# A fused attention and two-layer kernel whose setup loads x later, spreads its products differently and starts the second attention earlier

## The chip, the cores and the metric

The kernel runs on one core of one Trainium2 chip. The metric is device time in microseconds (us) of the whole launch. Before the change three runs gave a median of 1218.57 us (1217.18 to 1219.75).

## What is computed

From the reference, cut to what matters (B, H, S, Ns, D = 8, 8, 512, 32, 64):

```python
scores = scale * x @ state.T;  a = softmax(scores);   xread = a @ state
scores2 = scale * state @ x.T; a2 = softmax(scores2); sread = a2 @ x
x = concat([xread, sread], axis=2)          # 8 blocks of 512 + 32 rows, 512 wide
x = ((x @ w1) * (x @ w2) @ w3) @ w_out      # w1, w2: 512 x 1024; w3: 1024 x 1024; w_out: 1024 x 512
h = x @ w_in;  out = (h * clip(h + 3, 0, 6) / 6) @ w_out2
```

All tensors come in single precision; the weights are handed over as 64-bit words that the kernel converts itself.

## The kernel before, in words

**Setup.** Twenty units of 1 MB (128x4096 of 16 bits) are loaded by SyncE (SP), and ScalarE (ACT) and VectorE (DVE) turn each into a 128x1024 fp32 tile. `ORDER` (line 120) gives their kinds: units 0 to 7 alternate w_out (`o`) and the first half of w3 (`a`), 8 to 11 are the second half of w3 (`w`), 12 to 19 are w1 and w2 (`p`). `Pipe.pump` (line 194) does unit t: three DVE instructions (`ts`, `hd`, then a product, lines 164 to 166), a hook `inside(t)`, the last DVE instruction (line 168), then ACT's `hd` of unit t+1 (line 151) and SP's load of unit t+3 (three `raw` buffers, so a load waits for the product of the unit three before). After that `more(t)` issues what is written there for step t: loads of x (`load_x`), steps of the attention generator, ends of w3 rows (`w3_done`), products of w3 by w_out (`bulk_mm`, line 463, tiles `ps_w`), and from t = 15 on the work of block 0.

**The folded weight.** `bulk_mm(n)` takes up to n of the 64 fp32 products of w3 @ w_out; eight of them add up to one of eight rows m = 0 to 7 in a PSUM bank of four (`ps_w`). `w3_done(m)` splits row m into a high and a low part (`w3ph` by ACT, `w3pl` by DVE) and so frees the bank. Later products are done as three passes on such parts (`mm3`, lines 88 to 90).

**Attention of a block.** `attention(b, fine)` is a generator: load `xn`; `scores` 0 (line 237); out of it (`mr`, `sN`, `e`: lines 241 to 244); scores 1; out of it; `max_n` (286 to 289); `exp_n` (292, 294); `e2_t` 0 (transposes, line 252); `sum_n`; `e2_t` 1; `div_n`; `sread` (267); `turn` (306); `Ah`; `Al`. `step()` advances the oldest living generator by one piece. With `fine` true (the attentions of blocks 0 and 1) each of these is a step of its own. The results `Ah`, `Al` are what block b multiplies by.

**P.** Instead of x @ w1 the kernel forms P = state @ w1 (w2) for four parts v per block (`p_mm`, line 409, tiles `ps_p`, two PSUM banks of a second set of four) and splits it (`p_split`, tiles `ph`, `pl`).

**Block 0 inside the setup.** `early_mm(m)` (12 products into two banks `ps_ab`), `early_ab(m)` (`asb` by ACT, `ab` by DVE, then `abh` by ACT and `abl` by DVE) and `early_x2(m)` (12 products by w3's row m into `x`) do slots 0 to 3 of block 0 at t = 16 to 20. Slots 4 to 7 and the blocks after that go through `slot(b, m, ...)`, with one attention step ahead of `ab`'s parts (`before`) and one after (`mid_`).

**The second stream.** `stream2()` (line 475) is a generator that converts and splits the weights of the last layer during blocks 0 to 5; `ROOM` and, for block 0, `ROOM0` say how much of it each of a slot's two hooks may take. Its first step loads two units, its second is ACT's `hd` (line 489), its third DVE's `ts` (line 516).

All engines run in the order in which this program issues; nothing reorders it.

Of the kernel before, what the change touches and what calls it, by code (L numbers as in the profile page):

```python
# [19 lines left out]
def attn_moe_kernel(tc, xt_d, xn_d, bd_d, wa, wb, wc, wi, wo, out):  # L20
# [36 lines left out]
    def close_pool(key):  # L57
        es.pop(key).close()
# [4 lines left out]
    def acc_bank(name):  # L63
        return psum.tile([128, 512], F32, tag="acc", name=name, bufs=4)
# [55 lines left out]
    ORDER = "oaoaoaoawwwwpppppppp"  # L120

    ROOM = ((3, 3), (3, 4), (3, 3), (3, 3), (0, 1), (3, 3), (5, 5), (5, 6))
    ROOM0 = (None, None, None, None, (0, 0), (1, 2), (2, 3), (2, 3))


    class Pipe:
# [87 lines left out]
    def load_x(b):  # L214
        xr = att.tile([128, 4, 512], F32, tag="xr", name=f"xr{b}")
        br = mid.tile([128, 4, 64], F32, tag="br", name=f"br{b}", bufs=2)
        nc.sync.dma_start(out=br, in_=bd_d[b])
        nc.sync.dma_start(out=xr, in_=xt_d[b])
        x_t[b] = (xr, br)
# [153 lines left out]
    live = []  # L373

    def step():
        if live:
            try:
                next(live[0])
            except StopIteration:
                live.pop(0)  # L380
# [5 lines left out]
    with tc.manual_schedule():  # L386
# [26 lines left out]
        def p_split(v):  # L413
            ps = p_ps.pop(v)
            h, l = (main.tile([128, 2, 512], F32R, tag=f"p{hl}", name=f"p{hl}", bufs=2) for hl in "hl")
            for i in range(2):
                phl[v, i] = h[:, :, 256 * i:256 * i + 256], l[:, :, 256 * i:256 * i + 256]
            for c in range(2):
                rnd(h[:, c], ps[c], "A")
            for c in range(2):  # L420
                rest(l[:, c], ps[c], h[:, c], "V")

        def w3_out(m, ps):
            w3p_h[m], w3p_l[m] = w3p_tile("h", m), w3p_tile("l", m)
            rnd(w3p_h[m], ps, "A")
            rest(w3p_l[m], ps, w3p_h[m], "V")
# [31 lines left out]
        def bulk_mm(n):  # L458
            for _ in range(min(n, len(bulk))):
                t, m, k, o = bulk.pop(0)  # L460
                if k == 0:
                    w3_ps[m] = acc_bank(f"ps_w{m}")
                nc.tensor.matmul(w3_ps[m], t[:, o:o + 128], wout[k], start=k == 0, stop=k == M1 - 1)
# [98 lines left out]
        def w3_done(m):  # L562
            w3_out(m, w3_ps.pop(m))
# [24 lines left out]
        def x2_mm(blk, m, ab, n, es_):  # L588
            if m == 0 and es_[0] == 0:
                accs[blk] = [acc_bank(f"x2_{e}") for e in range(KD)]  # L590
            for e in es_:
                mm3(accs[blk][e][:, :n], w3p_h[m][:, e * 128:(e + 1) * 128], w3p_l[m][:, e * 128:(e + 1) * 128],
                    ab[0][:, :n], ab[1][:, :n], m == 0, m == M1 - 1)
# [140 lines left out]
        def early_x2(m):  # L734
            x2_mm(0, m, e_ab[m], 512, range(4))


        def early_ab(m):
            ab = ab_mul(*e_ps.pop(m), 512)
            hi = ab_hi(ab, 512)  # L740
            e_ab[m] = hi, ab_lo(ab, hi, 512)

        def inside(t):
            if t == 16:
                p_split(0)
            elif t > 16:
                if t == 17:
                    w3_done(7)
                early_ab(t - 17)
                if t == 17:  # L750
                    p_split(1)

        def more(t):
            if t == 1 or t == 12:
                load_x(t // 12)
            if t in (4, 18):
                live.append(attention(t // 18, True))
                step()
            for _ in range({5: 1, 6: 1, 7: 1, 8: 1, 10: 1, 11: 1, 12: 2, 13: 1, 19: 1}.get(t, 0)):
                step()  # L760
            for m in {9: (0, 1), 10: (2, 3), 11: (4,), 13: (5,), 15: (6,)}.get(t, ()):
                w3_done(m)
            if t == 15:
                p_mm(0)
            if t in (4, 5, 9, 10, 11):
                step()
            if t > 1 and ORDER[t] in "aw":
                w3u[ORDER[:t].count("a") + ORDER[:t].count("w")].mm()
            if t >= 16:
                early_mm(t - 16)  # L770
            bulk_mm(4 if t == 1 or t > 8 else 5 if t < 8 else 3)
            if t == 16:
                p_mm(1)
            if t >= 17:
                early_x2(t - 17)
            if t == 18:
                step()
            if t == 19:
                p_mm(2)

# [11 lines left out]
        early_ab(3)  # L792
        p_split(2)
        early_x2(3)
        second = stream2()
        for b in range(B):
            if 0 < b < B - 1:
                live.append(attention(b + 1))
            if b == B - 2:
                for _ in second:  # L800
                    pass
                close_pool("cvs")
                wsq = open_pool("wsq", bufs=1, side=right, reuse_waits="tile")
            if b == B - 1:
                xs_h, xs_l = xs_hl
                s_block()
                close_pool("wsq")
                close_pool("att")
                xb = open_pool("xb", bufs=1, side=right, reuse_waits="tile")
                first = combos(0)  # L810
            A = A_t.pop(b)
            for m in range(0 if b else 4, M1):
                if m == (6 if b else 5) and b + 2 < B:
                    load_x(b + 2)

                def pump(i):
                    nonlocal room
                    room += (ROOM if b else ROOM0)[m][i]
                    while room > 0:
                        room -= next(second, 99)  # L820

                def before():
                    step()
                    pump(0)

                vn = 4 * b + m // 2 + 1

                def mid_():
                    if vn < 4 * B and m % 2 == 0:
                        p_mm(vn)  # L830
                        p_split(vn)
                    step()
                    pump(1)
                slot(b, m, A, before, mid_)
                if b == 0:
                    step()
                if b == B - 2 and m >= 2:
                    if m == 2:
                        xs_r = wsq.tile([128, KD, SR], F32, name="xs_r")
                        n = (B - 1) * NS  # L840
                        nc.sync.dma_start(out=xs_r[:, :, :n], in_=xsd[:, :, :n])
                    ws_split(m - 2, [wsq.tile([128, 1024], F32R, tag=f"ws{hl}", name=f"ws{hl}", bufs=6) for hl in "hl"])
                if b == B - 1:
                    for _ in range(1 if m == 0 else 4):
                        next(first, None)
            drain_att()
# [476 lines left out]
```

## Time and profile before

| | value |
|---|---|
| median of 3 runs | 1218.57 us (1217.18 to 1219.75) |
| the profiled execution | 1216.74 us; its span, first to last instruction, 1214.9 us |
| TensorE (PE) busy | 1188.6 us, 98% of the span |
| VectorE busy | 861.2 us, 71% |
| ScalarE busy | 552.8 us, 46% |
| chain that ended last | PE 90%, DVE 7%, DMA 1%, ACT 1% |
| mean granted TensorE clock | 0.995 of full speed |

The shares are means over stages. A wait is read from the row of the instruction that waited: in brackets stands how long its engine sat idle before it, and who released it. A matmul's start times are exact, its end is modelled, so the distance from one start to the next is the better measure of one matmul.

### The profile page before, as it was taken

To read this page: it belongs to the slowest core of one execution; us is meant where nothing else is said; L and a number is where in the kernel's file an instruction comes from. 1 tells how busy PE (TensorE), PEld (TensorE's weight loads), DVE (VectorE), ACT (ScalarE), POOL (GpSimd) and SP (SyncE) were. 2 spreads that over 40 slices of the span, in tenths; PEclk is the share of its full clock that TensorE was granted. 3 is DMA by queue.
4 is the path that set the end of the run, shared out by engine and by line. 5 is a ranking of instruction groups with operands and counts; after the bars stand their busy time and mean duration, and the time that the engine had idled before them with its cause. 6 is when DMAs were issued, how large, how long until landed. Compare 5 with 4: busy or idle time off the path is not lost.

```text
span 1214.9 us, 17239 instructions
## 1 busy us (share of the span) xinstructions
PE 1188.6 (98%) x6734; PEld 945.8 (78%) x6734; DVE 861.2 (71%) x1230; ACT 552.8 (46%) x811; POOL 44.6 (4%) x59
## 2 busy tenths in 40 slices
PE   7898899999999999999999999999999999999998
PEld 4445677778777779978888888888888888888887
DVE  6986589888978664264678866688666886558483
ACT  3533455654645454244445434455344543334341
POOL 0000000000000000000101001010010100001100
PEclk9999899999999999999999999999999999999999
DMA  9761358675765511126899778898788986445973
GB/s 345 248 249 69 115 192 260 206 262 192 257 213 193 198 51 38 51 96 216 250 273 266 248 258 258 262 263 257 254 258 261 263 256 226 162 142 161 249 231 70
DMA packets 118930, 252.67 MB, mean 208 GB/s; under 512 B 45248, under 2 KB 63168, under 8 KB 112448
## 3 DMA queue, kind: packets, MB, share of 16 engines
q1 hardware_dynamic: 109552, 222.46, 53.9%
q0 software_dynamic: 7632, 27.79, 11.4%
q10 hardware_dynamic: 1664, 1.31, 0.3%
q8 instruction: 53, 0.87, 0.3%
q14 instruction: 29, 0.24, 0.1%
HBM read 182.39 MB, written 47.64 MB: 189 GB/s over the span
## 4 chain that ended last, share of the span: by engine, by line
PE 90%; DVE 7%; DMA 1%; ACT 1%; issue 0%; SPq 0%; ACTq 0%; DVEq 0%
PE ps L995 25%; PE ps_d L1157 25%; PE x L88 5%; PE x L89 5%; PE x L90 5%; PE ps_ab L88 5%; PE ps_ab L89 5%; PE ps_ab L90 5%; PE ps_p L409 3%; PE ps_hs L995 2%; PE ps_so L1170 2%; DMA raw<-in_wb_dram 1%; PE ps_r L267 1%; PE ps_s L237 1%; DVE t L168 1%; DVE big L168 1%
## 5 line engine op out<-in xcount | busy, mean ns | idle before, releaser
L995 PE MATMUL ps<-xc,wah 128*128 128x512 f32 x512 | 157.9, 389 | 0.0
L79 DVE TENSOR_TENSOR hlj<-g,hlj 128x1024 fp32r<-128x1024 f32 x84 | 102.2, 1217 | 35.6 <-ACT hlj L71 32.6
L925 ACT ACTIVATE rl<-c,half 128x512 f32<-128x512 f32 x96 | 69.5, 724 | 117.0 <-DVE c L895 68.1
L995 PE MATMUL ps<-xc,wbh 128*128 128x512 f32 x384 | 118.3, 389 | 0.0
L1157 PE MATMUL ps_d<-hlj,wah 128*128 128x512 f32 x384 | 118.2, 389 | 0.0
L88 PE MATMUL x<-abh,w3ph 128*128 128x512 f32 (+1 forms) x288 | 112.2, 390 | 0.0
L71 ACT ACTIVATE hlj<-g 128x1024 fp32r<-128x1024 f32 x84 | 88.5, 1057 | 50.7 <-PE ps_d L1157 45.2
L995 PEld LDWEIGHTS ps<-xc,wah 128*128 128x128 f32 x512 | 95.7, 188 | 19.5
L89 PE MATMUL x<-abl,w3ph 128*128 128x512 f32 (+1 forms) x288 | 109.3, 379 | 0.1
L90 PE MATMUL x<-abh,w3pl 128*128 128x512 f32 (+1 forms) x288 | 108.9, 378 | 0.0
L89 PE MATMUL ps_ab<-Al,ph 128*128 128x512 f32 x256 | 101.2, 395 | 2.4 <-DVE Al L79 2.4
L88 PE MATMUL ps_ab<-Ah,ph 128*128 128x512 f32 x256 | 102.7, 401 | 0.6 <-ACT Ah L71 0.4
L90 PE MATMUL ps_ab<-Ah,pl 128*128 128x512 f32 x256 | 101.0, 395 | 0.0
L995 PE MATMUL ps<-xc,wal 128*128 128x512 f32 x256 | 99.6, 389 | 0.0
L1157 PE MATMUL ps_d<-hlj,wbh 128*128 128x512 f32 x288 | 88.7, 389 | 0.0
L71 ACT ACTIVATE abh<-ab 128x512 fp32r<-128x512 f32 (+1 forms) x72 | 43.7, 607 | 89.0 <-DVE ab L573 89.0
L1157 PEld LDWEIGHTS ps_d<-hlj,wah 128*128 128x128 f32 x384 | 72.1, 188 | 15.0
L995 PEld LDWEIGHTS ps<-xc,wbh 128*128 128x128 f32 x384 | 72.0, 188 | 15.0
L573 DVE TENSOR_TENSOR ab<-ps_ab,asb 128x512 f32<-128x512 f32 x64 | 44.0, 688 | 49.1 <-PE ps_ab L90 42.1
L963 POOL DMA_DIRECT2D g<-g x41 | 35.6, 869 | 1086.6 <-DVE c L895 578.4
L995 PE MATMUL ps<-xc,wbl 128*128 128x512 f32 x192 | 74.7, 389 | 0.0
L1157 PE MATMUL ps_d<-hlj,wal 128*128 128x512 f32 x192 | 74.7, 389 | 0.0
(170 smaller groups left out, 2356.6 us busy)
## 6 DMA issues: line engine op xcount, KB each, us to landing
g<-g POOLq DMA_DIRECT2D x41, 512.0 KB, 7.0
wah<-swih SPq DMA_DIRECT2D x32, 512.0 KB, 4.5
wal<-swil SPq DMA_DIRECT2D x32, 512.0 KB, 5.9
wah<-swoh SPq DMA_DIRECT2D x32, 512.0 KB, 4.5
wal<-swol SPq DMA_DIRECT2D x32, 512.0 KB, 5.5
wbh<-swih SPq DMA_DIRECT2D x32, 384.0 KB, 5.0
wbl<-swil SPq DMA_DIRECT2D x32, 384.0 KB, 5.3
wbh<-swoh SPq DMA_DIRECT2D x32, 384.0 KB, 5.6
```

The lines of the kernel that those rows point to most:

```text
L71: nc.scalar.activation(out=out_, in_=in_, func=AF.Copy)
L79: e.tensor_tensor(out=out_, in0=in_, in1=hi.bitcast(F32), op=ALU.subtract)
L88: nc.tensor.matmul(ps, lh, rh, start=first, stop=False)
L89: nc.tensor.matmul(ps, lh, rl, start=False, stop=False)
L90: nc.tensor.matmul(ps, ll, rh, start=False, stop=last)
L168: v.tensor_tensor(out=w, in0=w, in1=hd.bitcast(BF16), op=ALU.add)
L409: nc.tensor.matmul(ps[c][32 * q:32 * q + 32, 256 * i:256 * i + 256], st_t[b][r, 2 * c + j, 32 * k:32 * k + 32], w12[mm // 2, 2 * c + j][r, ...
L573: nc.vector.tensor_tensor(out=ab[:, :n], in0=psb[:, :n], in1=a[:, :n], op=ALU.mult)
L925: nc.scalar.activation(out=rl, in_=c, func=AF.Relu, bias=half, scale=sign / 6.0)
L963: nc.gpsimd.dma_start(out=to, in_=of, accum_op=ALU.add)
L995: nc.tensor.matmul(ps, u[:, k, :], v[:, k, :], start=first and k == 0 and i == 0, stop=k == 1 and i == 2, skip_group_check=True)
L1157: nc.tensor.matmul(d[name][q][:, f], a, x[:, k, f], start=i < 3 and n == 0 and z == 0, stop=n == NG - 1 and z == 2, skip_group_check=True)
```

## The change

Only the order of the setup and of block 0's hooks changes; no computation is added or dropped. x of block 0 is loaded after unit 3's conversion instead of after unit 1's, and its attention begins at t = 6 instead of 4. The products of w3 per step are given by a table (`BULK`), so that all 64 are issued by t = 15 (before: 4 per step from t = 9 on, the last four at t = 16, behind `early_mm(0)`). The end of row 7 (`w3_done(7)`) moves from inside conversion 17 to step 16. The two first parts of P are formed at t = 15 together, where the second came at t = 16 behind `early_mm(0)`. The attention of block 1 begins at t = 16 instead of 18 and takes its steps in other places: both score steps and `max_n` come before the setup's end, `e2_t` in slots 4 and 5, `turn` in slot 6, `Ah` and `Al` in slot 7, and the extra step after each slot of block 0 goes. The second stream's two first loads are issued before slot 4, and `ROOM0` lets block 0 take 16 units of it instead of 13.

```diff
-    ROOM0 = (None, None, None, None, (0, 0), (1, 2), (2, 3), (2, 3))
+    ROOM0 = (None, None, None, None, (0, 1), (2, 2), (2, 3), (3, 3))
...
             elif t > 16:
-                if t == 17:
-                    w3_done(7)
                 early_ab(t - 17)
...
+        PRE = {7: 1, 8: 1, 9: 1, 10: 1, 12: 1, 13: 1, 14: 2, 15: 1, 18: 1, 19: 1}
+        POST = {6: 1, 7: 1, 11: 1, 12: 1, 13: 1, 17: 1, 18: 1, 19: 1}
+        BULK = {1: 4, 2: 0, 3: 5, 4: 3, 5: 5, 6: 3, 7: 5, 8: 3, 15: 2}
+        DONE = {9: (0, 1), 10: (2, 3), 11: (4,), 13: (5,), 14: (6,), 16: (7,)}
+
         def more(t):
-            if t == 1 or t == 12:
+            if t == 3 or t == 12:
                 load_x(t // 12)
-            if t in (4, 18):
-                live.append(attention(t // 18, True))
+            if t in (6, 16):
+                live.append(attention(t // 16, True))
                 step()
-            for _ in range({5: 1, 6: 1, 7: 1, 8: 1, 10: 1, 11: 1, 12: 2, 13: 1, 19: 1}.get(t, 0)):
+            for _ in range(PRE.get(t, 0)):
                 step()
-            for m in {9: (0, 1), 10: (2, 3), 11: (4,), 13: (5,), 15: (6,)}.get(t, ()):
+            for m in DONE.get(t, ()):
                 w3_done(m)
             if t == 15:
                 p_mm(0)
-            if t in (4, 5, 9, 10, 11):
-                step()
...
             if t >= 16:
                 early_mm(t - 16)
-            bulk_mm(4 if t == 1 or t > 8 else 5 if t < 8 else 3)
-            if t == 16:
+            for _ in range(POST.get(t, 0)):
+                step()
+            bulk_mm(BULK.get(t, 5))
+            if t == 15:
                 p_mm(1)
             if t >= 17:
                 early_x2(t - 17)
-            if t == 18:
-                step()
             if t == 19:
                 p_mm(2)
...
         early_x2(3)
+        step()
         second = stream2()
+        next(second)
...
                 slot(b, m, A, before, mid_)
-                if b == 0:
-                    step()
```

The queue of SP at the start of the setup (`raw` a unit, `br` and `xr` the x of block 0, `wa` w_out, `wb` w3), before:

```order
L139 DMA raw<-in_wb_dram 128x4096
L139 DMA raw<-in_wa_dram 128x4096
L217 DMA br_189<-in_bd_dram 128x256
L218 DMA xr_188<-in_xt_dram 128x2048
L139 DMA raw<-in_wb_dram 128x4096
L139 DMA raw<-in_wa_dram 128x4096
L139 DMA raw<-in_wb_dram 128x4096
```

and with the change, from the same place on:

```order
L139 DMA raw<-in_wb_dram 128x4096
L139 DMA raw<-in_wa_dram 128x4096
L139 DMA raw<-in_wb_dram 128x4096
L139 DMA raw<-in_wa_dram 128x4096
L217 DMA br_213<-in_bd_dram 128x256
L218 DMA xr_212<-in_xt_dram 128x2048
L139 DMA raw<-in_wb_dram 128x4096 x3
```

The first row is unit 3. x now stands behind units 5 and 6 and ahead of unit 7; it stood behind unit 4.

VectorE at the end of the setup, from slot 2's `ab` (out of `ps_ab_660`) to slot 3's (out of `ps_ab_707`) and behind it; `big_689` is unit 19, before:

```order
L573 TENSOR_TENSOR ab<-ps_ab_660,asb 128x512
L79 TENSOR_TENSOR abl<-ab,abh 128x512
L168 TENSOR_TENSOR big_689<-big_689,hd 128x1024
L241 TENSOR_REDUCE mr<-ps_s 128x1
L242 TENSOR_SCALAR mr<-mr 128x1
L243 STREAM_TRANSPOSE sN<-ps_s 128x512
L573 TENSOR_TENSOR ab<-ps_ab_707,asb 128x512
L79 TENSOR_TENSOR abl<-ab,abh 128x512
L79 TENSOR_TENSOR pl<-ps_p,ph 128x512 x2
```

and with the change, where `ps_ab_667` and `ps_ab_714` are the products of slots 2 and 3 and `big_696` is unit 19:

```order
L573 TENSOR_TENSOR ab<-ps_ab_667,asb 128x512
L79 TENSOR_TENSOR abl<-ab,abh 128x512
L168 TENSOR_TENSOR big_696<-big_696,hd 128x1024
L241 TENSOR_REDUCE mr<-ps_s 128x1
L242 TENSOR_SCALAR mr<-mr 128x1
L243 STREAM_TRANSPOSE sN<-ps_s 128x512
L286 TENSOR_REDUCE mx<-sN 128x32
L287 TENSOR_TENSOR sN<-sN,mx 128x1024
L288 TENSOR_SCALAR mr<-mr 128x2
L289 RECIPROCAL mr<-mr 128x2
L573 TENSOR_TENSOR ab<-ps_ab_714,asb 128x512
L79 TENSOR_TENSOR abl<-ab,abh 128x512
```

Here the second scores of block 1 and `max_n` (lines 286 to 289) now stand ahead of slot 3's `ab`; before, only the first scores did.

ScalarE in slots 4 and 5 of block 0 (`asb`, `abh` of a slot, `ph` a part of P, `sN` and `e` block 1's softmax, `hd` the second stream's first unit, `e2t` the evicted transposes), before:

```order
L571 COPY asb<-ps_ab_783 128x512
L71 ACTIVATE abh<-ab 128x512
L71 ACTIVATE ph<-ps_p 128x512 x2
L244 ACTIVATE e_657,mr<-ps_s,mr 128x512
L571 COPY asb<-ps_ab_845 128x512
L292 ACTIVATE sN<-sN 128x1024
L294 ACTIVATE e_657<-e_657,mr 128x512 x2
L489 ACTIVATE hd<-raw 128x1024
L71 ACTIVATE abh<-ab 128x512
L257 COPY e2t<-ps_e 128x512
```

and with the change:

```order
L292 ACTIVATE sN<-sN 128x1024
L294 ACTIVATE e_571<-e_571,mr 128x512 x2
L571 COPY asb<-ps_ab_802 128x512
L71 ACTIVATE abh<-ab 128x512
L71 ACTIVATE ph<-ps_p 128x512 x2
L257 COPY e2t<-ps_e 128x512
L489 ACTIVATE hd<-raw 128x1024
L571 COPY asb<-ps_ab_867 128x512
L71 ACTIVATE abh<-ab 128x512
L257 COPY e2t<-ps_e 128x512
```

The exponentials of block 1 (lines 292, 294) stood behind slot 5's `asb`; now they stand ahead of slot 4's, and the transposes' eviction comes before slot 5.

## Rows read from the trace of the kernel before

**Rows 1.** Busy time by stage: PE, PEld, DVE, ACT, POOL, then PE's clock, DMA share, GB/s.

```profile
150.00:300.00 150.00, 150.00 (x1157) 114.51 (x1148) 128.49 (x208) 84.63 (x138) 0.00 (x0) 1.00 0.67 216
```

**Rows 2.** The same view, four stretches of 10 us in the setup and block 0.

```profile
20.00:30.00 10.00, 9.32 (x25) 3.31 (x25) 7.69 (x11) 2.97 (x3) 0.00 (x0) 1.00 1.01 425
...
70.00:80.00 10.00, 7.36 (x45) 2.75 (x44) 9.86 (x13) 3.73 (x5) 0.00 (x0) 1.00 0.90 306
...
120.00:130.00 10.00, 7.53 (x25) 5.94 (x26) 5.84 (x10) 5.44 (x8) 0.00 (x0) 0.66 0.62 233
...
140.00:150.00 10.00, 7.18 (x30) 4.95 (x36) 5.66 (x11) 3.97 (x5) 0.00 (x0) 0.83 0.22 93
```

**Rows 3.** ACT in order of time, units 4 to 6: start, us, engine, line, operation.

```profile
19.55 1.13 ACT L151 ACTIVATE hd<-raw 128x1024 bf16<-128x1024 bf16 x1 [2.25 <-DMA raw<-in_wa_dram]
24.86 1.14 ACT L151 ACTIVATE hd<-raw 128x1024 bf16<-128x1024 bf16 x1 [4.17 <-DMA raw<-in_wb_dram]
27.34 1.14 ACT L151 ACTIVATE hd<-raw 128x1024 bf16<-128x1024 bf16 x1 [1.34 <-DMA raw<-in_wa_dram]
```

**Rows 4.** VectorE in order of time, first half of the setup.

```profile
26.04 0.43 DVE L164 TENSOR_SCALAR ts<-hd 128x1024 uint16<-128x1024 uint16 x1 [2.04 <-ACT hd L151]
...
35.23 0.38 DVE L164 TENSOR_SCALAR ts<-hd 128x1024 uint16<-128x1024 uint16 x1
...
38.38 1.21 DVE L286 TENSOR_REDUCE mx<-sN 128x32 f32<-128x1024 f32 x1
...
41.05 0.41 DVE L164 TENSOR_SCALAR ts<-hd 128x1024 uint16<-128x1024 uint16 x1
...
47.42 1.28 DVE L79 TENSOR_TENSOR w3pl<-ps_w,w3ph 128x512 fp32r<-128x512 f32 x2
```

**Rows 5.** PE in order of time, setup: a product of w3 is two passes.

```profile
45.48 0.60 PE L252 MATMUL ps_e<-ident,e 128*128 128x128 f32 x4
48.16 2.41 PE L463 MATMUL ps_w<-wo,t 128*128 128x512 f32 x5 [2.07 <-DVE w3pl L79]
...
55.66 2.06 PE L267 MATMUL ps_r<-e2t,xn 128*64 128x32 f32 x64
57.65 14.00 PE L463 MATMUL ps_w<-wo,t 128*128 128x512 f32 x32
```

**Rows 6.** PE's waits in the first 150 us: total, times, longest.

```profile
PE ps_p L409 <- DVE big L168: 2.6, 2, 2.5
```

**Rows 7.** PE in order of time, block 0: a score, slot 3's x2, first transposes.

```profile
98.75 1.08 PE L237 MATMUL ps_s<-xr,br 128*64 128x512 f32 x4
...
106.49 0.50 PE L88 MATMUL x<-abh,w3ph 128*128 128x512 f32 x1
...
122.33 1.51 PE L252 MATMUL ps_e<-ident,e 128*128 128x128 f32 x4 [4.55 <-ACT e L294]
```

**Rows 8.** PE in order of time, first matmuls of block 1.

```profile
141.26 0.49 PE L88 MATMUL ps_ab<-Ah,ph 128*128 128x512 f32 x1 [0.44 <-ACT Ah L71]
144.14 0.50 PE L89 MATMUL ps_ab<-Al,ph 128*128 128x512 f32 x1 [2.38 <-DVE Al L79]
```

**Rows 9.** VectorE in order of time, second half of the setup and block 0.

```profile
67.22 1.22 DVE L79 TENSOR_TENSOR Al<-aT,Ah 128x1024 fp32r<-128x1024 f32 x1
...
72.14 0.42 DVE L164 TENSOR_SCALAR ts<-hd 128x1024 uint16<-128x1024 uint16 x1
...
87.00 0.69 DVE L79 TENSOR_TENSOR w3pl<-ps_w,w3ph 128x512 fp32r<-128x512 f32 x1 [4.80 <-ACT w3ph L71]
...
102.05 0.68 DVE L241 TENSOR_REDUCE mr<-ps_s 128x1 f32<-128x512 f32 x1
...
104.93 0.69 DVE L573 TENSOR_TENSOR ab<-ps_ab,asb 128x512 f32<-128x512 f32 x1 [1.38 <-ACT asb L571]
...
138.82 1.30 DVE L306 STREAM_TRANSPOSE aT<-sN 128x512 f32<-128x512 f32 x2
...
141.47 0.68 DVE L79 TENSOR_TENSOR abl<-ab,abh 128x512 fp32r<-128x512 f32 x1
```

## The prediction, made before the change was run

> **What bounds the kernel now.** I read the busy time by stage first. From 150 us on PE is busy in all of every stretch, at full clock, while VectorE has 21.5 us of 150 free [rows 1]: there nothing waits that PE waits for. So the end is set by when PE gets through the first 150 us, and one us of PE idleness that goes there is one us of time, unless VectorE cannot follow. The second view is the same table for stretches of the setup: there PE has holes, VectorE is full at 70 to 80 us (9.86 of 10), and the clock is not 1.00 at 120 to 130 and at 140 to 150 us [rows 2]. The third view is the order of time on ACT, VectorE and PE, for what ended each hole [rows 3 to 9].
>
> PE's holes behind its first product of row 4 of the folded weight, 48.16 us [rows 5], are four. It waits 2.6 us for the conversions before P's first part [rows 6]; 4.55 us for block 1's exponentials before the first transposes [rows 7]; 0.44 us for `Ah` and 2.38 us for `Al` of block 1 [rows 8]. After the 4.55 us the granted clock is at its lower level, 1.2 GHz, for a while: a mean of 0.66 over 10 us is 3.4 us lost, of which some 0.3 fall in the wait itself, so 3.1. After the other, 0.83 over 10 us: 1.7 us [rows 2]. The wait of 2.07 us ahead of 48.16 ends with `w3pl` of row 0, which frees a PSUM bank [rows 5]; that moment hangs on VectorE alone.
>
> **The change, part by part.** All instructions stay; PE's work is the same. I count by how much PE's stream moves, and take that from the time.
>
> *x two conversions later.* Transfers of this queue land one behind the other: unit 5 was there 5.31 us after unit 4 (19.55 to 24.86, ACT's starts, which ended its waits for them), with x between them, unit 6 2.48 us after unit 5 [rows 3]. So a unit takes 2.48 us and x 2.83. With x behind unit 6, unit 5 lands at 22.0, unit 6 at 24.5, x at 27.3, unit 7 at 29.8, and unit 7's `hd` (1.14 us [rows 3]) is there at 31.0. VectorE's wait of 2.04 us at unit 5 [rows 4] goes: unit 5 starts at 24.0, unit 7 would start two units of 3.15 us later (35.23 to 38.38 [rows 4]), at 30.3, and waits 0.7. What else VectorE does up to `w3pl` of row 0 (47.42 [rows 4]) is the same: two score steps, `max_n`, units up to 9. Gain 1.4 us: PE starts row 4 at 46.8.
> The page "DMA: Bandwidth & Descriptors" of the Trainium skill, section "Queues, rings and completion order", says that each DMA engine takes one queue's descriptors in ring order but need not finish them so. The spacing above agrees with the order. If x shared the engines with unit 6 instead, unit 6 would land up to 2.83 us later, VectorE would wait about 1.5 us there, and the whole sum below would be some 0.8 smaller.
>
> *First transposes behind row 4.* One `e2_t` stood ahead of 48.16 (0.60 us, next to a wait [rows 5]); it now comes behind. Cost 0.5 us.
>
> *Products and P.* PE now has 30 products, two `e2_t` and `sread` between 46.8 and P's first part. A product takes 0.875 us (32 passes, 16 products, in 14.00), `sread` 2.06 [rows 5]: row 6 ends at 46.8 + 21.0 + 1.0 + 2.1 = 70.9, P's part 0 can start at 76.1. VectorE reaches `w3pl` of row 6 at 72.14 (unit 15's start before) less 1.4 and less `Al`'s 1.2, which now stands behind unit 15: 69.5 [rows 9]. There it waits for row 6 and ACT's half, until 71.4: a new wait of 1.9 us on VectorE. Unit 15 then ends at 71.4 + 0.6 + 3.15 = 75.2, ahead of PE. So the 2.6 us [rows 6] go, as long as PE is late there by its 0.9 us. Their cover is the products; without it the old wait is back in part.
>
> *Row 7's end at step 16.* VectorE idled 4.80 us before this `w3pl` [rows 9], since its product stood on PE behind slot 0. All products now come before. That idleness goes, and pays for what is moved in.
>
> *Second attention sooner.* Ahead of slot 3's `ab` VectorE now also does the second score step (1.5 us: 102.05 to 104.93 less 1.38 of idleness [rows 9]) and `max_n` (2.67 us: 38.38 to 41.05 [rows 4]). Its `ab` stood at 104.93 [rows 9]; now 104.93 - 4.80 - 1.38 - 1.4 + 1.5 + 2.7 + 1.9 = 103.5. Before, PE began slot 3's x2 at 106.49 [rows 7], 1.56 us after that `ab`; so VectorE allows it at 105.0. PE comes there at 106.49 less 1.4 and 2.6, plus 0.5 and plus one score more ahead of it (1.0 [rows 7]), so 104.0, and some 0.3 later for bank waits. It waits about 0.7 us; ACT now has an exponential ahead of that slot's `asb`, so I take **1.0**. Bounds: 0, and 2.4, the largest short wait for VectorE in this part [rows 8].
> The 4.55 us before the first transposes go, with the 3.1 us at half speed: the exponentials stand a slot sooner on ACT, and PE still has slot 3's x2 and slot 4's product ahead, 24 passes or 6 us (106.49 to 117.78 held 36 passes, a score and a part of P in 11.3 us). Gain 7.65.
> `turn` and the second stream's combination, 2.65 us (138.82 to 141.47 [rows 9]), stood between slot 7's `ab` and block 1's `Al`; now they stand ahead of that `ab`, and `Al` comes inside slot 7. Of 2.82 us of waiting 0.2 would be left if VectorE arrived on time; with `turn` and the combination just ahead of `ab` it will be somewhat late: I take 1.0, between 0 and 2.82. The 1.7 us at half speed behind go. Net gain 3.5.
>
> *Second stream's loads sooner, ROOM0 up by 3.* The first transfer is then there before ACT's `hd`; three units are work that block 1 no longer does. No PE wait is tied to either: nothing, covered by the 21.5 us free on VectorE [rows 1]; without that cover at most their VectorE time.
>
> *Banks.* P's two parts stand together, so slots 0 and 1 take their banks from parts that VectorE has only just split: short waits, three of 0.2, by a guess between 0 and the 0.44 of [rows 8] each. Cost 0.6.
>
> **Sum.** 1.4 - 0.5 + 2.6 - 1.0 + 7.65 + 3.5 - 0.6 = 13.05, so 13.0 us less. The profiled execution took 1216.74 us, 1.83 below the median shown and 0.44 below the fastest run; I take the 13.0 from the median: 1218.57 - 13.0 = **1205.6 us**.
>
> **The rivals.**
> 1. *The clock falls at a new place.* In favour: it fell after 4.55 us and after 2.82 us of idle PE. Against: a stop of PE of 2.07 us (ahead of 48.16) and the 2.6 us near 75 us went by at 1.00 [rows 2, 5, 6]; my new waits are 1 us. If the wait at slot 3's x2 or at block 1's start is long enough, 1.7 to 3.1 us come back, with up to 1.8 more of waiting: 1207.3 to 1210.5. The page "TensorE: Matmul & The Clock Gate" of the Trainium skill, section "HAM oscillation — how this bites in real kernels", makes idle gaps in the matmul stream the cause of such falls; the four waits named bear out that long gaps do it, not that every gap does.
> 2. *The lead is handed back in blocks 0 to 5.* VectorE has the same work in less time. For it: 128.49 of 150 us busy [rows 1], and the second stream stands one piece further on against the slots, so that its pieces meet the attention at other places. Against: 21.5 us free per 150. If a wait of about 1 us appears per block, 5 to 8 us are lost: 1210.6 to 1213.6.
> 3. *Slower.* VectorE arrives late at slot 3's `ab`, the one place where all the moved work stands in a row. The price: a 4.55 us wait cost 7.65 with the clock, 1.7 per us. It would eat 13.0 and 2.4 more if VectorE came 9 us later than I count, say if the setup's loads fell behind x and `xn` by 9 us: 1221 or more. Against: two such transfers together are about 5.5 us, and units need 2.48 us each for 3.15 us of conversion, so a delay heals.
> 4. *No change*, lead lost altogether to 2 and 1 together: 1216.2 to 1221.
>
> **How the numbers follow.** About 0.2% (2.4 us) is what a measurement of this kernel can tell from no change. My forecast, 11 to 15.5 us less, has 0.62 (up to 15.7 with all three new waits at nothing); rival 1 0.18; rival 2 0.13; no change 0.04; slower 0.03. Faster by more than 0.2% is the first three, 0.93. The range: low 1202.5, the sum with the new waits at nothing (1202.9) and a little for the runs' own spread; high 1211.5, the clock falling once (3.1), `Al` as late as before (1.8) and the gain from x gone (1.4), 1205.6 + 6.3 = 1211.9; that leaves out about half of rival 2, rivals 3 and 4.
>
> **What would show it.** Right: VectorE no longer waits at unit 5, and less than 1 us at unit 7; PE starts row 4 near 46.8; no PE wait before P's first part; VectorE waits some 2 us at row 6's `w3pl`, and not before row 7's; PE's wait before the first transposes is gone, clock 1.00 at 110 to 130 us; `Al` is waited for 1 us or less; block 1's first product starts near 131.3 (140.82, when PE was free for it, less the 9.55 of the terms before it), and from its `Al` on PE stays 13 us ahead. Wrong: a PE wait of 2 us or more at slot 3's x2, half speed behind it, or PE waits beyond 150 us.

## The result and the profile after

Four runs of the changed kernel had a median of 1207.33 us (1205.57 to 1209.6), the kernel before beside them 1218.7. The ratio is 0.9909 (95% interval 0.9889 to 0.9929), some 11 us less. The forecast was 1205.6 in a range of 1202.5 to 1211.5. The profiled execution took 1205.57 us (before: 1216.74), its span is 1203.8 (before: 1214.9).

Busy time by stage of the changed kernel, columns as in [rows 1, 2]:

```profile
20.00:30.00 10.00, 9.40 (x15) 4.10 (x16) 9.29 (x13) 3.05 (x3) 0.00 (x0) 0.66 0.98 388
70.00:80.00 10.00, 10.00 (x54) 4.39 (x53) 8.26 (x12) 3.61 (x6) 0.00 (x0) 1.00 0.66 215
120.00:130.00 10.00, 10.00 (x126) 7.69 (x125) 8.61 (x16) 4.90 (x8) 0.00 (x0) 1.00 0.34 113
140.00:150.00 10.00, 10.00 (x46) 8.29 (x45) 9.22 (x17) 5.86 (x12) 0.00 (x0) 1.00 0.73 291
150.00:300.00 150.00, 148.74 (x1152) 114.14 (x1152) 127.08 (x202) 81.99 (x132) 0.00 (x0) 1.00 0.67 223
```

The holes at 70 to 80, 120 to 130 and 140 to 150 us are filled and the clock is 1.00 there. Two things are new in this execution: the clock was at half speed for part of 20 to 30 us (the last section shows that the setup of before can do that too), and PE was not busy for 1.26 us of the stretch from 150 on.

PE in order of time, the places of [rows 5 to 8]:

```profile
48.80 8.85 PE L463 MATMUL ps_w<-wo,t 128*128 128x512 f32 x20 [1.84 <-DVE w3pl L79]
...
77.81 1.09 PE L409 MATMUL ps_p<-big,br 64*32 64x256 f32 x32
78.83 1.99 PE L463 MATMUL ps_w<-wo,t 128*128 128x512 f32 x4
...
106.56 0.49 PE L88 MATMUL x<-abh,w3ph 128*128 128x512 f32 x1 [1.46 <-ACT abh L71]
107.29 0.50 PE L89 MATMUL x<-abl,w3ph 128*128 128x512 f32 x1 [0.23 <-DVE abl L79]
112.65 0.60 PE L252 MATMUL ps_e<-ident,e 128*128 128x128 f32 x4
...
133.02 0.50 PE L89 MATMUL ps_ab<-Al,ph 128*128 128x512 f32 x1 [0.59 <-DVE Al L79]
...
219.40 0.66 PE L252 MATMUL ps_e<-ident,e 128*128 128x128 f32 x4 [1.26 <-DVE ab L573]
```

Row 4 starts 0.64 us later than before, not 1.4 sooner. P's first part, the first transposes and `Ah` are not waited for any more. Slot 3's x2 waits 1.69 us, `Al` 0.59. The last row is block 1's second `e2_t`: it takes its bank from a slot's products, and their `ab` came late.

VectorE and ACT in the setup, the places of [rows 3, 4, 9]; ACT's two rows are `hd` of units 6 and 7:

```profile
26.34 1.15 ACT L151 ACTIVATE hd<-raw 128x1024 bf16<-128x1024 bf16 x1 [3.10 <-DMA raw<-in_wa_dram]
31.89 1.13 ACT L151 ACTIVATE hd<-raw 128x1024 bf16<-128x1024 bf16 x1 [4.40 <-DMA raw<-in_wb_dram]
...
33.05 0.43 DVE L164 TENSOR_SCALAR ts<-hd 128x1024 uint16<-128x1024 uint16 x1 [2.24 <-ACT hd L151]
...
48.07 1.27 DVE L79 TENSOR_TENSOR w3pl<-ps_w,w3ph 128x512 fp32r<-128x512 f32 x2
...
73.39 0.69 DVE L79 TENSOR_TENSOR w3pl<-ps_w,w3ph 128x512 fp32r<-128x512 f32 x1 [1.64 <-ACT w3ph L71]
...
82.59 0.68 DVE L79 TENSOR_TENSOR w3pl<-ps_w,w3ph 128x512 fp32r<-128x512 f32 x1
...
105.16 0.69 DVE L573 TENSOR_TENSOR ab<-ps_ab,asb 128x512 f32<-128x512 f32 x1
```

VectorE's wait at unit 5 is gone, and one of 2.24 us stands at unit 7 (33.05). The wait at row 6's `w3pl` is there (73.39), the one of 4.80 at row 7's is not (82.59).

### The profile page after: what moved, and what is told of

Read it like the earlier page. It is cut to its first block, busy times and chain, and to the rows that moved or that the text cites. A ratio compares the mean times of both kernels' runs of the same rounds, so it can differ in the third digit from the quotient of the medians.

```text
span 1203.8 us, 17243 instructions
## 1 busy us (share of the span) xinstructions
PE 1185.6 (98%) x6734; PEld 944.4 (78%) x6734; DVE 862.1 (72%) x1230; ACT 553.5 (46%) x811; POOL 44.6 (4%) x59
## 4 chain that ended last, share of the span: by engine, by line
PE 91%; DVE 5%; DMA 2%; ACT 1%; issue 0%; SPq 0%; ACTq 0%
PE ps L996 25%; PE ps_d L1158 25%; PE x L88 5%; PE x L89 5%; PE x L90 5%; PE ps_ab L88 4%; PE ps_ab L89 4%; PE ps_ab L90 4%; PE ps_p L409 2%; PE ps_w L463 2%; PE ps_hs L996 2%; PE ps_so L1171 2%; DMA raw<-in_wb_dram 1%; PE ps_r L267 1%; PE ps_s L237 1%; DMA swih<-sh 1%
```

## The experiments

Each run has its own runs of the kernel before beside it; the ratio is to those. A difference between two runs of under 1.5 us is read from the traces, since single runs of one kernel spread over 1 to 6 us. Unless a sentence says otherwise, rows are those of the view in order of time of the run being told: start, us, engine, line, operation, and in brackets how long the engine was idle before and who ended it.

### The two halves of the change

**Setup only**: the changed kernel with the second attention's steps, the second stream's first piece and `ROOM0` as before. The diffs of this part are cut to their ends: the attention's other steps move with them.

```diff
-            if t in (6, 16):
-                live.append(attention(t // 16, True))
+            if t in (6, 18):
+                live.append(attention(t // 18, True))
...
-        step()
         second = stream2()
-        next(second)
```

> The changed kernel with the second attention and the second stream back at their places of before: only the setup's part is left (x and the first attention later, products, ends of rows, P's two parts together). Theory A, the gain is nearly all the second attention's: PE comes to slot 3's x2 some 2.4 us sooner than before (after reached it at 105.1 with one score of 1.0 more done, before at 106.49), no wait for P's first part, but the wait of about 4.5 us before the first transposes, the half speed behind it and the wait of 2.8 us at block 1's start are all still there. 2 to 3 us less than before: about 1216. Rival B, the setup's part carries a good part of the gain by itself, since VectorE no longer idles 4.8 us at row 7: those waits shrink with it, 5 us or more less than before: under 1214.

Measured: 1216.65 us, ratio 0.9984 (0.9974 to 0.9993), about 1.9 us: theory A. PE's waits of block 0 stood where they were before. The gain is one of the medians: the profiled execution, 1216.72 us, is no faster than that of the kernel before, and lost some 3 us to the clock at row 4, as a later part shows.

```profile
122.99 0.33 PE L252 MATMUL ps_e<-ident,e 128*128 128x128 f32 x1 [4.55 <-ACT e L294]
...
143.79 0.80 PE L89 MATMUL ps_ab<-Al,ph 128*128 128x512 f32 x1 [2.38 <-DVE Al L79]
```

**Second only**: the kernel before with the other half.

```diff
-            if t in (4, 18):
-                live.append(attention(t // 18, True))
+            if t in (4, 16):
+                live.append(attention(t // 16, True))
...
         early_x2(3)
+        step()
         second = stream2()
+        next(second)
```

> The kernel before with only the second attention (steps from t = 16 on) and the second stream's first piece sooner, the setup as before. Theory A: the 4.55 us before the first transposes, the 3.1 us at half speed and most of block 1's 2.82 + 1.7 us go as in the changed kernel; VectorE now has the second score step and max_n (4.2 us, less 1.38 of idleness) ahead of slot 3's ab, and PE waits 1.5 to 3 us at slot 3's x2. 7.5 to 9.5 us less than before: 1209 to 1211. Rival B, without the setup's part VectorE still idles 4.8 us at row 7's w3pl and comes so late to slot 3 that the wait there is 4 us or more and the clock falls behind it: 5 us less or under, 1213.5 or more.

Measured: 1208.84 us, ratio 0.9923 (0.9908 to 0.9938), about 9.4 us.

```profile
76.37 1.06 PE L409 MATMUL ps_p<-big,br 64*32 64x256 f32 x22 [1.56 <-DVE big L168]
109.96 0.50 PE L88 MATMUL x<-abh,w3ph 128*128 128x512 f32 x1 [1.41 <-ACT abh L71]
137.99 0.50 PE L89 MATMUL ps_ab<-Al,ph 128*128 128x512 f32 x1 [0.59 <-DVE Al L79]
```

The price at slot 3's x2 is 1.41 and 0.23 us and no more, so the idleness of 4.8 us at row 7, still there in this run, was not needed to pay for the moved steps: the rival falls. 1.9 and 9.4 add up to the whole gain of 11 within the intervals.

### The second stream's first transfers

**Stream late**: the changed kernel with `ROOM0` of before and without `next(second)`, the early first piece.

```diff
-    ROOM0 = (None, None, None, None, (0, 1), (2, 2), (2, 3), (3, 3))
+    ROOM0 = (None, None, None, None, (0, 0), (1, 2), (2, 3), (2, 3))
...
         second = stream2()
-        next(second)
```

> The changed kernel with the second stream where it was before (ROOM0 of before, no first piece at the start). Theory A (rival 2 of the prediction): the wait of 1.26 us for slot's ab at block 1's second e2_t, where VectorE did a combination of four instructions just ahead of that ab, comes from the stream standing further on against the slots; with the old place it goes, PE is busy 150.0 of 150 from 150 to 300 us, and no new wait of over 0.5 comes before: 1.3 us less than the changed kernel, about 1206. Rival B: VectorE now waits about 3 us for the stream's first hd around 115 to 120 us as it did before (3.07), slots 5 to 7 get late, and block 1's Al is waited for 1.5 us or more: same time or slower.

Measured: 1214.24 us, ratio 0.9966 (0.9955 to 0.9978), 7 us worse than the change. Theory A's wait in block 1 went (150.00 of 150 us busy), but the rival's direction held, by far more than the 1.5 us of waiting that it named, and the place is ACT:

```profile
118.76 0.59 ACT L257 COPY e2t<-ps_e 128x512 f32<-128x512 f32 x1
119.37 0.59 ACT L571 COPY asb<-ps_ab 128x512 f32<-128x512 f32 x1
125.68 1.10 ACT L489 ACTIVATE hd<-raw 128x1024 bf16<-128x1024 bf16 x1 [5.72 <-DMA raw<-in_wi_dram]
126.69 0.61 ACT L71 ACTIVATE abh<-ab 128x512 fp32r<-128x512 f32 x1
127.20 0.56 ACT L257 COPY e2t<-ps_e 128x512 f32<-128x512 f32 x1
```

ACT stands 5.72 us at the `hd` that needs the first transfer, which SP issued at 118.79, behind block 2's x. Slot 5's `abh` and the second `e2t` are queued behind it. PE then waits 3.46 us in the middle of `sread` for that `e2t`:

```profile
127.82 3.20 PE L267 MATMUL ps_r<-e2t,xn 128*64 128x32 f32 x56 [3.46 <-ACT e2t L257]
```

Before the change the same `hd` had waited 0.48 us: the transfer was issued at 115.76, ACT was busy with the exponentials until 122.9, and `hd` started at 123.37. Once the exponentials come a slot sooner, that cover is gone. SP's and ACT's rows of the kernel before:

```profile
115.76 0.33 SPq L483 DMA_DIRECT2D raw<-in_wi_dram  x1
...
123.37 1.13 ACT L489 ACTIVATE hd<-raw 128x1024 bf16<-128x1024 bf16 x1 [0.48 <-DMA raw<-in_wi_dram]
```

**First only** takes one of these two edits back, `next(second)`, and leaves `ROOM0` at its values of before.

```diff
-    ROOM0 = (None, None, None, None, (0, 1), (2, 2), (2, 3), (3, 3))
+    ROOM0 = (None, None, None, None, (0, 0), (1, 2), (2, 3), (2, 3))
```

> The changed kernel with ROOM0 of before, but with the second stream's first piece (its two first transfers) early, as in the change: the run stream_late with one of its two edits taken back. Theory A, what cost 7 us there is the late first transfer alone (issued at 118.8 us instead of 98.0, ACT stood 5.72 us at the hd that needs it, with abh, e2t and asb queued behind): ACT does not wait for that transfer here, PE does not wait at sread, and the time is the changed kernel's or better by up to 1.3 us (no wait for ab at block 1's second e2_t): 1206 to 1207.5. Rival B, the pieces moved by ROOM0 matter as well, since VectorE and ACT meet slots 5 to 7 in another order: some of the 7 us stays, 1209 or more.

Measured: 1207.06 us, ratio 0.9918 (0.9903 to 0.9932), the changed kernel's time. ACT's `hd` has no wait:

```profile
118.61 1.13 ACT L489 ACTIVATE hd<-raw 128x1024 bf16<-128x1024 bf16 x1
```

So the early transfer alone is worth the 7 us, and `ROOM0` alone makes the wait in block 1: PE is busy 150.00 of 150 us here too, at the price of 1.10 us of waiting for `Al` instead of 0.59.

### Where x is loaded

**x at 1** and **x at 5** are the changed kernel with x in another place of SP's queue.

```diff
-            if t == 3 or t == 12:
+            if t == 1 or t == 12:
```

> The changed kernel with x loaded at t = 1 again, all else as changed. Theory A, the place of x among units 5 to 7 is worth nothing, since VectorE pays for the transfer wherever it stands there: wait of 2.0 us at unit 5, under 0.8 at unit 7, PE starts row 4 at 48.2 to 49.2, time within 0.6 us of the changed kernel. Rival B, what the prediction said: x behind unit 6 saves 1.4 us, so this one is 1.4 us slower than the changed kernel and PE starts row 4 at about 50. The half speed at 20 to 26 us should be gone if it came with x's new place.

Measured: 1206.2 us, ratio 0.9901 (0.9885 to 0.9916), the same as the change. VectorE's wait is back at unit 5 and gone at unit 7, and row 0's `w3pl` stands 0.52 us sooner than in the changed kernel. The 1.4 us that rival B gave x's place are not there. The half speed did not go with x either: the mean clock from 20 to 30 us is 0.83 here.

```profile
26.15 0.43 DVE L164 TENSOR_SCALAR ts<-hd 128x1024 uint16<-128x1024 uint16 x1 [2.05 <-ACT hd L151]
...
47.55 1.27 DVE L79 TENSOR_TENSOR w3pl<-ps_w,w3ph 128x512 fp32r<-128x512 f32 x2
```

> The changed kernel with x loaded at t = 5, behind unit 8 on SP's queue. Theory A, x costs VectorE a wait only while loads are what VectorE waits for, and by unit 8 they are not: the wait of 2.24 us at unit 7 shrinks to 0.8 or less, no wait over 0.5 at units 8 and 9, w3pl of row 0 and with it PE's row 4 come 1.5 to 2 us sooner (46.8 to 47.3). Further on that is kept, since row 6 and P's part 0 hang on PE there: 1.2 to 2 us less than the changed kernel, about 1205.5. Rival B, the wait only moves on again (to unit 8 or 9, or to PE's first score product, which stood at 35.03 and now needs x by then): same time as the changed kernel within 0.6.

Measured: 1207.27 us, ratio 0.9907 (0.9891 to 0.9924), the same again; its edit is `t == 5`. VectorE's wait at unit 7 is 1.32 us, and it has two new ones, 2.18 and 0.71 us, for the scores, since PE now waits for x:

```profile
36.63 1.14 PE L237 MATMUL ps_s<-xr,br 128*64 128x512 f32 x4 [3.00 <-DMA xr<-in_xt_dram]
```

The rival holds here: none of the three places of x is faster than another by more than the runs spread. But x is not all that VectorE waits for. With x two units behind it, unit 6 came no sooner than with x right behind it in the changed kernel. ACT's `hd` of unit 6 in this run (26.34 in the changed kernel):

```profile
26.50 1.16 ACT L151 ACTIVATE hd<-raw 128x1024 bf16<-128x1024 bf16 x1 [2.66 <-DMA raw<-in_wa_dram]
```

Its load was issued at 19.37 us here and at 19.36 there, when the product of unit 3 had freed the buffer, and took 7.0 and 6.9 us to land. Units 4 to 8 took 6.3 to 7.7 us in these two runs where x did not stand ahead of them, and unit 7 took 8.9 with x ahead of it. So of the 2.24 us at unit 7 a good part, 1.32, is there without x in front. From 20 to 30 us the DMA engines were 98% busy in the changed kernel and 91% here.

### P's second part

**P1 later** takes alone the one part of the change that no other run isolates.

```diff
-            if t == 15:
+            if t == 16:
                 p_mm(1)
```

> The changed kernel with P's second part one step later (t = 16, behind slot 0's products on PE, as before the change), the only part of the change that no run so far has taken alone. Theory A, it is worth nothing either way: its split on VectorE stands at t = 17 in both; PE's one bank wait of 0.39 us at block 1's first score goes and nothing comes in its place, time within 0.6 us of the changed kernel (1206.7 to 1207.9). Rival B, the early place hides something: ACT's and VectorE's split of this part now waits for PE, slot 2's products come late, and PE waits 1 us or more in slots 1 to 3: 1208.3 or more.

Measured: 1207.98 us, ratio 0.9922 (0.9908 to 0.9936), within 0.7 of the change. No PE wait in slots 1 to 2 is over 0.3 us (a bank wait of 0.29 instead of 0.39), and slot 3's x2 waits 1.54 and 0.22. This part does nothing that can be measured.

### The waits that were left

**Max0 behind** and **max1 behind** move one `max_n` each in the changed kernel, **both max** moves both.

```diff
-        PRE = {7: 1, 8: 1, 9: 1, 10: 1, 12: 1, 13: 1, 14: 2, 15: 1, 18: 1, 19: 1}
-        POST = {6: 1, 7: 1, 11: 1, 12: 1, 13: 1, 17: 1, 18: 1, 19: 1}
+        PRE = {7: 1, 8: 1, 10: 1, 12: 1, 13: 1, 14: 2, 15: 1, 18: 1, 19: 1}
+        POST = {6: 1, 7: 1, 9: 1, 11: 1, 12: 1, 13: 1, 17: 1, 18: 1}
...
         p_split(2)
+        step()
         early_x2(3)
```

(The 9 is max0's edit; the 19 and the added `step()` are max1's.)

> The changed kernel with max_n of the first attention (2.66 us on VectorE, from 45.41 to 48.07) moved from ahead of the ends of rows 0 and 1 to behind them. Theory A, PE's start of row 4 hangs on VectorE's w3pl of row 0 alone: w3pl stands at 45.4, PE's wait of 1.84 us before row 4 goes, row 4 starts at 47.0, and with no wait there the clock cannot fall behind it (it did in the runs setup_only, second_only and x_at_1, after 2.07 to 3.30 us of waiting, and did not in before and after). VectorE had 1.64 us of waiting at row 6's w3pl to give, so 1.6 us less than the changed kernel up to block 1, about 1205.7, and more against executions in which the clock fell. Rival B, VectorE is late at P's first part or at slot 3 by the work it now does later: PE waits there for what it saved, same time as the changed kernel within 0.6.

Measured: 1205.27 us, ratio 0.9894 (0.9880 to 0.9908), 2 us less than the change by the medians. In its trace both theories are half right: row 4 starts at 45.83 after 0.52 us of waiting, and P's first part waits 1.51 us for unit 15 again, so that `Al`'s first product is only 0.33 us ahead of the changed kernel's (132.69 against 133.02). Why the medians show more is the subject of the part on the clock.

```profile
45.83 8.85 PE L463 MATMUL ps_w<-wo,t 128*128 128x512 f32 x20 [0.52 <-DVE w3pl L79]
...
76.99 1.06 PE L409 MATMUL ps_p<-big,br 64*32 64x256 f32 x22 [1.51 <-DVE big L168]
```

> The changed kernel with max_n of the second attention behind slot 3's ab, abl and pl instead of ahead of them. Theory A: VectorE's lateness at slot 3's ab is these 2.67 us; PE's waits of 1.46 and 0.23 us at slot 3's x2 go (0 to 0.3 left), the exponentials come some 1 us later on ACT but PE has 24 passes ahead of the first transposes, so no wait over 0.5 there: 1.2 to 1.7 us less than the changed kernel, about 1205.9. Rival B: what is saved at x2 is paid at the first transposes or at slot 4: same time within 0.6.

Measured: 1207.01 us, ratio 0.9909 (0.9895 to 0.9924), no less than the change by the medians. In its trace the wait for `abh` at slot 3's x2 is gone (0.22 us for `abl` left) and 0.26 us appear at the first transposes; but this execution lost more at row 4, as the part on the clock shows.

> The changed kernel with both of these max_n moved (first attention's behind the ends of rows 0 and 1, second attention's behind slot 3's ab). If both savings are PE's own and independent, no PE wait before row 4 and under 0.4 at slot 3's x2: 2.8 to 3.3 us less than the changed kernel, about 1204.2, and block 1's first product with Al at about 130. If VectorE is the bound behind slot 3, the waits come back at the first transposes, at slot 4 or at Al: 1.6 us less or under.

Measured: 1204.23 us, ratio 0.9885 (0.9871 to 0.9899), the time that independent savings were to give (the two profiled executions differ by 2.3 us, the medians by 3.1): no wait before row 4, 0.23 at slot 3's x2. P's first part still waits 0.88 us, and `Al`'s first product stands at 131.14 against 133.02.

**Row 6 late** adds to both max that row 6 ends behind unit 15, **row 6 room** adds `ROOM0` of before to that.

```diff
-        DONE = {9: (0, 1), 10: (2, 3), 11: (4,), 13: (5,), 14: (6,), 16: (7,)}
+        DONE = {9: (0, 1), 10: (2, 3), 11: (4,), 13: (5,), 15: (6,), 16: (7,)}
```

> The run both_max with the end of row 6 moved behind unit 15 (t = 15). There VectorE waits 1.61 us for row 6's products ahead of unit 15, and then PE waits 0.88 us for unit 15 at P's first part. Theory A: VectorE does unit 15 in that wait, no PE wait before P's parts, 0.9 us less than both_max (1203.3), and up to 0.4 more if the short waits for VectorE in slots 0 to 3 go with it. Rival B, VectorE's time behind P's parts is what binds up to slot 3 or the split of P is now later by the moved w3pl: PE waits there, same time as both_max within 0.4.

Measured: 1202.46 us, ratio 0.9878 (0.9860 to 0.9897). PE waits for no part of P, and its longest wait between row 4 and block 1 is the 0.59 us for `Al`.

> row6_late with ROOM0 of before, the first transfers early. If theory A of first_only holds, the wait for ab in block 1 (0.7 us in both_max) goes too: 1202.6. If its rival holds, it is slower than row6_late by what first_only is slower than the changed kernel.

Measured: 1201.76 us, ratio 0.9875 (0.9856 to 0.9894). The wait in block 1 is gone (150.00 of 150 us busy), `Al` is waited for 1.10 us. By the medians it is the fastest version here, though not clear of row 6 late, 15 us less than the kernel before and some 4 less than the change by the ratios (0.9875 against 0.9909).

### Row 4 and the clock

Every profile has one execution, and in all of them the clock can be read behind the wait for row 0's `w3pl`. In this table stands PE's wait just ahead of row 4 and the mean granted clock from 50 to 55 us.

| run | wait, us | clock |
|---|---|---|
| both max | under 0.2 | 1.00 |
| max0 behind, row 6 late, row 6 room | 0.52, 0.58, 0.65 | 1.00 each |
| x at 5 | 0.96 | 1.00 |
| after | 1.84 | 1.00 |
| before | 2.07 | 1.00 |
| second only | 2.07 | 0.73 |
| P1 later, x at 1 | 2.19, 2.38 | 0.66, 0.77 |
| max1 behind, stream late | 3.09, 3.17 | 0.76, 0.78 |
| setup only | 3.30 | 0.50 |
| first only | 5.27 | 0.72 |

At this place no wait of up to 1.84 us was followed by the lower level of 1.2 GHz, and of eight waits from 2.07 on seven were. (In x at 5 the clock fell earlier, behind the 3.00 us for x: 0.75 from 35 to 40 us.) The price is read where 20 passes of rows 4 and 5 stand in a row, 8.85 us at full speed (in max0 behind and in the changed kernel, above). Here are max1 behind and, below it, setup only:

```profile
48.63 10.55 PE L463 MATMUL ps_w<-wo,t 128*128 128x512 f32 x20 [3.09 <-DVE w3pl L79]
49.05 11.80 PE L463 MATMUL ps_w<-wo,t 128*128 128x512 f32 x20 [3.30 <-DVE w3pl L79]
```

That is 1.7 and 3.0 us in an execution. It need not be made up later: in P1 later, where the 20 passes took 10.55 too, `Al`'s first product stood at 134.70 against 133.02.

Six of these executions run the same program up to row 4: after, P1 later, max1 behind, stream late, setup only, first only. In all six row 4 starts at 48.63 to 49.24 us, when row 0's `w3pl` is done. What differs is when PE was done with the products before it: the mean clock from 20 to 30 us was 0.66, 0.69, 0.83, 0.83, 0.83 and 1.00, and the wait 1.84, 2.19, 3.09, 3.17, 3.30 and 5.27, in that order. Where PE ran slower at first it idled less here. The profiled execution of the changed kernel, also the fastest of its four, is the only one of the six that kept full speed behind this wait; the other five lost 1.6 to 3.0 us over the 20 passes. So its row of 1.84 us and 1.00 is a lucky one.

This is the likely reason why max0 behind gains 2 us by the medians and 0.33 in the traces: its wait is 0.52 us, and the clock behind it stays up. The mean granted clock of the whole executions agrees, 0.994 to 0.996 in the changed kernel's four and 0.997 to 0.998 in max0 behind's four; where the changed kernel's other three fell was not seen. Max1 behind is best compared with P1 later, which lost the same at row 4: `Al` at 133.88 against 134.70. Why it gains nothing by the medians stays open.

## Why the prediction was right, and where its steps were not

The time came out 1.7 us above the forecast; "from `Al` on PE 13 us ahead" was nearly so: block 1's next part of P started at 137.10 against 149.85, a lead of 12.75. Within that the terms shift.

- **x two conversions later: wrong, 1.4 forecast, nothing gained.** Row 4 started 0.64 us later than in the profile of before; it stood at 48.16 and 49.05 in the two executions with the setup of before (before, second only) and at 48.63 to 49.24 in the six that have the changed one unaltered up to there. The step that failed is "With x behind unit 6, unit 5 lands at 22.0, unit 6 at 24.5, x at 27.3, unit 7 at 29.8". Unit 5's `hd` did start at 22.09, but unit 6's at 26.34 and unit 7's at 31.89. The spacing of 2.48 us was read where unit 5 stood behind x and unit 6's load had long been issued when unit 5 landed. Here unit 6's load was issued at 19.36, when its buffer came free, and landed 6.9 us later; 24.5 would have been 5.1. x behind it is not the cause, since the same load took 7.0 us in x at 5. Behind unit 6 the transfers followed as the prediction had them: x landed at 29.1 and unit 7 at 31.8, so the 1.8 us of unit 6 came to unit 7, and the wait there was 2.24 us instead of 0.7. That x shared the engines with unit 6, which the prediction allowed for, is not what happened. The page "DMA: Bandwidth & Descriptors" of the Trainium skill, section "Queues, rings and completion order", from which the prediction took that an engine takes a queue's descriptors in ring order but need not finish them so, agrees in its first half: unit 6, x and unit 7 landed in the order of their issue. No run here shows the second half.

The view of the DMA issues of the changed kernel, 15 to 40 us; the first row is unit 6, and the last number is the time from issue to landing:

```profile
raw<-in_wa_dram SPq DMA_DIRECT2D x1, 1024.0 KB, 6.9
xr<-in_xt_dram SPq DMA_DIRECT2D x1, 1024.0 KB, 8.9
```

- **`e2_t` behind row 4:** 0.5, as costed; nothing contradicts it.
- **P's first part: right in kind, 2.6 forecast, some 3.9 there.** The hole was read from the idle column [rows 6]. From start to start it was longer: P's first part began at 71.58 and the products behind it at 76.46, 4.88 us, against 77.81 to 78.83 now, 1.02. The ends of matmuls are modelled, so a wait between short ones is partly counted as busy. VectorE's new wait at row 6's `w3pl` was 1.64 (forecast 1.9), and row 7's 4.80 went. PE in the kernel before:

```profile
71.58 0.62 PE L409 MATMUL ps_p<-big,br 64*32 64x256 f32 x2
72.37 0.64 PE L409 MATMUL ps_p<-big,br 64*32 64x256 f32 x8 [0.18 <-DVE big L168]
75.47 1.06 PE L409 MATMUL ps_p<-big,br 64*32 64x256 f32 x22 [2.46 <-DVE big L168]
76.46 3.70 PE L463 MATMUL ps_w<-wo,t 128*128 128x512 f32 x8
```

- **Slot 3's x2: too small, 1.0 forecast, 1.69 measured.** `ab` stood at 105.16, not 103.5: the term carried the 1.4 of x's place that was not there. Max1 behind shows that `max_n` ahead of `ab` is what costs it.
- **Block 1's transposes and `Al`: right, 11.15 forecast, 12.05 measured.** PE was 0.7 us ahead at slot 3's x2 (a score of 1.0 more done, 0.07 and 0.23 us later) and 12.75 at block 1's next part of P. No half speed was left; `Al` was waited for 0.59 instead of 1.0.
- **The second stream at nothing: the reasoning was wrong, though not the sum.** "No PE wait is tied to either: nothing, covered by the 21.5 us free on VectorE" looked at VectorE alone. The early transfer is worth 7 us here (stream late, first only), because ACT works in order and `hd` would have held `abh` and `e2t`. The terms of 7.65 and 3.5 were right only because the change moved the transfer along. The row that would have told it was there before: ACT's `hd` at 123.37, already waiting 0.48 for its transfer behind exponentials that were about to move away.
- **Banks: 0.6 forecast;** one wait of 0.39 us at block 1's first score was found.
- **Rival 2 happened once.** The lead of 12.75 shrank by 1.26 at block 1's second `e2_t`, where the second stream's combination (four instructions, 1.5 us) stood just ahead of the `ab` it waits for. First only shows `ROOM0` as its cause. No block after it waits, so the rival's price of 5 to 8 us did not come. The prediction had named a PE wait beyond 150 us as a sign of being wrong; this one is it.
- **Rival 1 did not decide,** but the evidence against it ("2.07 us went by at 1.00") was a single execution; by the table above the same 2.07 us went the other way in second only, and five of the six executions of the changed setup lost 1.6 to 3.0 us at row 4. The rule of the page "TensorE: Matmul & The Clock Gate" of the Trainium skill, section "HAM oscillation — how this bites in real kernels", that gaps in the matmul stream make the clock fall, agrees with seven of the eight waits from 2.07 us on.

The total is in part luck: x's 1.4 that did not come, 0.6 of a later row 4, 0.7 more at slot 3 and 1.26 in block 1 are set against 1.3 more at P's first part and 0.9 more at the transposes and `Al`, neither of which was foreseen. 11.65 us of lead are there at VectorE's last instruction (1198.71 against 1210.36); the spans differ by 11.1, since the last output transfer ended half a microsecond later behind it than before.

## What to carry to other kernels

When a step is moved sooner on an engine that works in order, look at what it used to cover there: an instruction behind it that waits for a transfer becomes the next stop, and the transfer has to be issued earlier by as much. Before counting on a transfer that moves within a queue, see when the loads around it can be issued at all: unit 6 could not be issued before its buffer was free and landed 7 us after that, with x right behind it or two units away. Read a wait in more than one execution: the same program idled 1.84 us here once and 5.27 us another time. And before moving a whole stage, look for the one long instruction group that stands ahead of the end of an accumulation that frees a bank: here exchanging `max_n` with it (2 us by the medians, probably most of it the clock) gave as much as the setup's whole rearrangement (1.9).

## What the runs showed of the hardware that was not expected

The same idleness of PE does not always end at the same clock. Behind the wait for unit 3, up to about 20.6 us, the granted clock was 1.00 from 20 to 30 us in the kernel before (3.63 us of idleness at its end) and in first only (3.21), and 0.66 in the changed kernel (3.18). In the fourteen profiles of this case eleven have 3.16 to 3.63 us of idleness there; behind it the mean clock from 20 to 30 us was 1.00 in two, 0.83 in seven, and 0.66 and 0.69 in two. Second only, with the setup of before, and x at 1 are among the seven, so neither the change nor x's place decides it. The products behind the wait, in the changed kernel:

```profile
20.60 14.50 PE L463 MATMUL ps_w<-wo,t 128*128 128x512 f32 x26 [3.18 <-DVE t L168]
```

and in first only:

```profile
20.34 11.66 PE L463 MATMUL ps_w<-wo,t 128*128 128x512 f32 x26 [3.21 <-DVE t L168]
```

The same 26 passes took 14.50 and 11.66 us. It cost nothing by itself, since PE had 1.84 us to wait before row 4 in the one and 5.27 in the other; the longer wait was then the one with the lower clock behind it. What decides between the two levels at the same idleness, no run here shows.
